# Scores of a chunked linear attention in four 64-column tiles, with the step halves of four heads swapped

## The chip, the cores and the metric

The kernel runs on one core of a Trainium2 chip. The metric is the time of one execution on the device in microseconds (us). The engines are named as in the profile: PE (TensorE; PEld is its weight load), DVE (VectorE), ACT (ScalarE), POOL (GpSimd), SP (SyncE, which here only issues DMAs).

## The reference

A layer of linear attention with a decay (RWKV5) feeds a gated feed-forward block. All arrays are float32.

```
r, k, v: [4 batches, 8 heads, 768 steps, 48]     w, u: [8, 48], w in 0.85 to 0.95
for t in steps:
    cur   = (u * k_t) outer v_t
    y_t   = r_t @ (state + cur)
    state = w * state + k_t outer v_t
x   = y as [3072 tokens, 384]
out = (silu(x @ w_gate) * (x @ w_val)) @ w_out    # w_gate, w_val: 384 x 1536, w_out: 1536 x 384
```

The loop over steps is a matrix product in pieces. Within 128 steps, y_t is a sum over the earlier steps s < t of (r_t . decayed k_s) v_s, plus the own step with u in place of the decay, plus r_t times the state that the 128 steps began with.

## The kernel before

**Items.** The attention is cut into 24 items: 6 chunks of 128 steps times 4 batches, numbered i = 4c + b. An item has 8 heads, in 4 pairs; head e of a pair lies in rows 64e to 64e+47 of a transposed tile. Each item goes through these steps:

- `load(i)` (L118 to L122) brings k and r, one DMA each, with the steps on the 128 partitions and heads and dimensions along the rows (tiles `k_ld`, `r_ld`; `hats` for the first four items). `load_v(i)` (L124 to L131) brings v in two DMAs, one for each e.
- POOL multiplies r, k and u (`own_product`, L234 and L235; tile `rk`), and DVE sums that over the dimensions (`own_sum`, L240; tile `du`). This is the own-step term of each head.
- POOL multiplies k and r by tables of powers of w (`scale_k` L307, `scale_r` L310; tables `kscale` and `rscale`, one row for each step of the chunk, both part of the tile `scales`). They are made once by `natural_tables` (L312 to L317).
- `turn(i)` (L343 to L353) transposes both for i < 12: PE writes tile `tp`, and ACT copies it to `kT` and `rT` (DVE for i < 4). From item 12 on, sixteen DMAs on SP move 32x32 blocks about (`move_blocks`, L355 to L373) and DVE turns each (`turn_blocks`, L379).
- `scores(i)` (L385 to L404) multiplies, for each head, the 48 rows of `kT` (128 keys, the stationary operand) with the 48 rows of `rT` (128 query steps, the moving operand): 8 matmuls into two PSUM tiles `s_ps`, one for each e. The result has keys on partitions and queries on columns, and only the part with key before query is wanted. `diagonal(i)` writes the own-step terms on the diagonal of the tile `At`, zero elsewhere (ACT L328, POOL L335). Then DVE copies `s_ps` into `At` where a mask of 128x128 says key < query (copy_predicated, L398).
- `outputs(i)` (L406 to L430) makes y in PSUM tile `y_ps`: for each 32 output rows it adds v times `At`, and the state `Z` times `rT`, in four column tiles of 32. ACT copies the result to `xT`.
- `update(i)` (L432 to L454) multiplies k and v over the steps (`u_ps`, four column tiles) and adds to the state (DVE, then POOL by a decay).

A matmul of an operand of 48 rows and 128 columns uses a part of the array only; the two heads of a pair lie in different rows, so they run side by side. Where this text speaks of a tile of the array, it means such a part, by rows and columns.

**Weights.** The three weight matrices come in 18 chunks of 768 KB (`load_weights`, L154 to L161, tile `w_bits`, three buffers). Each chunk is rounded by ACT (L179, L185) and DVE, and put together by POOL (L222). ACT's rounding of a chunk stands in the same order of instructions as its copies of `kT`, `rT`, and `xT`.

**Feed-forward.** `gate_value` (L464) makes the first groups of tokens, two recursive schemes with fewer products (L539 and L720) the rest. Their pieces wait in a list and are put between the attention's steps by `feed` and `gaps`.

**What sets the order.** Each engine works through its instructions in order, and the order is written out by hand (L976 to L1114): first items 0 to 3 with the weights, then a loop over s = 4 to 25. In it, loop step s does the loads of item s+3, v of item s+1, the scaling of item s+1, the turn of item s, the scores of item s-1 and the outputs and update of item s-2 (of item s-2 directly behind the scores of s-1 from s = 12 on). The DMAs of k, r, v, the weights and the block moves are all issued by SP, in this one order, each waiting for its own destination to be free.

In the built program every DMA of SP also waits for a semaphore of the DMA issued eight before it, so that there are at most eight in flight; that is so before and after the change.

Of the kernel before, what the change touches and what calls it, by code (L numbers as in the profile page):

```python
# [9 lines left out]
FP32 = mybir.dt.float32  # L10
INT32 = mybir.dt.int32
# [4 lines left out]
P = 128  # L16
# [6 lines left out]
def fast(  # L23
# [39 lines left out]
    ps_a = ctx.enter_context(tc.tile_pool(name="ps_a", bufs=4, space=bass.MemoryType.PSUM))  # L63
# [8 lines left out]
    bad = cst.tile([P, HP], FP32, name="bad")  # L72
    held = cst.tile([P, HP], FP32, name="held")
    badc = cst.tile([P, 1], FP32, name="badc")
    ones = cst.tile([P, 1], FP32, name="ones")
    ident = cst.tile([P, P], FP32, name="ident")
    mask = cst.tile([P, P], FP32, name="mask")
# [12 lines left out]
    free = deque(banks[:2])  # L90

# [25 lines left out]

    def load(i):  # L118
        c, b = divmod(i, B)
        rows = slice(P * c, P * (c + 1))  # L120
        for src, dst in zip((k, r), raw(i)):
            sp.dma_start(out=dst, in_=src[b, :, rows, :].rearrange("h t d -> t h d"))  # L122

    def load_v(i):  # L124
        c, b = divmod(i, B)
        rows = slice(P * c, P * (c + 1))
        for e in range(2):
            sp.dma_start(
                out=v_ld[i % 4][:, :, 64 * e : 64 * e + D],
                in_=v[b, :, rows, :].rearrange("(a e) t d -> e t a d", e=2)[e],  # L130
            )  # L131
# [133 lines left out]
    def warm(n):  # L265

        ps = ps_a.tile([P, HP, P], FP32, name="warm", tag="a")
        for _ in range(n):
            pe.matmul(ps[:, 0, :], ident[:], ident[:], start=True, stop=True)
# [6 lines left out]
        base=0, pattern=[[1, P]], channel_multiplier=-1,  # L276
    )
    dve.tensor_scalar(held[:], wcol[:], W_LOW, W_HIGH, ALU.max, ALU.min)
# [23 lines left out]
    def at(i, a):  # L302

        return HP - 1 - a if i >= BLOCKS and i % 2 == 0 else a

    def scale_k(i):
        pool.tensor_mul(khat[i % 4][:, :, 0:D], raw(i)[0], kscale)  # L307
# [4 lines left out]
    def natural_tables():  # L312
        for t, dst in ((pw[:, :, 1 : P + 1], kscale), (pv, rscale)):
            t_ps = ps_a.tile([P, HP, P], FP32, name="t_ps", tag="a")
            for a in range(HP):
                pe.transpose(t_ps[:, a, :], t[:, a, :], ident[:])
            act.copy(dst, t_ps[:].rearrange("p a (e x) -> p (a e) x", e=2)[:, :, 0:D])  # L317
# [25 lines left out]
    def turn(i):  # L343
        kr = khat[i % 4], rhat_of(i)
        tps = [ps_a.tile([P, HP, P], FP32, name="tp", tag="a") for _ in kr]
        turned[i] = three.tile([P, HP, P], FP32, name="rT", tag="rT")
        for tp, t, dst, table in zip(tps, kr, (kT[i % 2], turned[i]), (pw[:, :, 1 : P + 1], pv)):
            for a in range(HP):
                pe.transpose(tp[:, a, :], pair(t, a), ident[:])  # L349
            if i < 4:  # L350
                dve.tensor_mul(dst[:], tp[:], table)
            else:
                act.copy(dst[:], tp[:])  # L353
# [31 lines left out]
    def scores(i):  # L385

        while lazy:
            lazy.popleft()()
        ps = [ps_a.tile([P, HP, P], FP32, name="s_ps", tag="a") for _ in range(2)]
        for a in range(HP):  # L390
            for e in range(2):
                rows = slice(64 * e, 64 * e + D)
                pe.matmul(  # L393
                    ps[e][:, a, :], kT[i % 2][rows, at(i, a), :], turned[i][rows, at(i, a), :],
                    start=True, stop=True, skip_group_check=True,
                )
        for e in range(2):
            lazy.append(lambda e=e: dve.copy_predicated(  # L398
                At[i % 2][:].rearrange("p (a e) t -> p a e t", e=2)[:, :, e],
                mask[:].bitcast(INT32).unsqueeze(1).to_broadcast([P, HP, P]), ps[e][:],  # L400
            ))
        lazy.popleft()()
        if i < BLOCKS:
            lazy.popleft()()  # L404

    def outputs(i):  # L406

        c, b = divmod(i, B)  # L410
        A, vl, z = At[i % 2], v_ld[i % 4], Z[b]
        rT = turned.pop(i)
        ps = ps_a.tile([P, CC, P], FP32, name="y_ps", tag="a")
        cols = [[] for _ in range(4)]
        for m in range(4 * CC):
            (cc, q), (a, s) = divmod(m, 4), divmod(m, 3)
            each = [(z[0:R2, a, 32 * s : 32 * s + 32], rT[0:R2, at(i, a), :])] if c > 0 else []
            if s < 2:
                each.append((vl[:, a, 32 * s : 32 * s + 32], A[:, 2 * a, :]))
            if s > 0:  # L420
                each.append((vl[:, a, 32 * s + 16 : 32 * s + 48], A[:, 2 * a + 1, :]))
            cols[q] += [(cc, x, n == 0, n == len(each) - 1) for n, x in enumerate(each)]
        for n in range(len(cols[0])):
            for q in range(4):
                cc, x, start, stop = cols[q][n]
                pe.matmul(  # L426
                    ps[32 * q : 32 * q + 32, cc, :], *x,
                    start=start, stop=stop, skip_group_check=True,
                )
        act.copy(xT[:, i % NX, :, :], ps[:])  # L430

    def update(i):  # L432
# [4 lines left out]
        ps = ps_a.tile([P, HP, D], FP32, name="u_ps", tag="a")  # L437
# [398 lines left out]
    def three_units(g):  # L836
# [8 lines left out]
        def bank(chain):  # L845
            return wide[chain][:]

        def open_(chain):
            if chain in ("l4", "l2"):
                return take()  # L850
            return ps_a.tile([P, 4 * P], FP32, name=f"c_{chain}", tag="a")

        def later(at, do, out, *args):
            todo.append((at, lambda: do(out, *(bank(a) if isinstance(a, str) else a for a in args))))  # L854

# [9 lines left out]
        for t in range(4):  # L865
# [16 lines left out]
            later(z + 9.6, act.copy, y, "y")  # L882
            later(z + 10.4, dve.tensor_add, c[5], q10, "l5")
            later(z + (11.55 if t == 3 else 10.5), dve.tensor_add, c[2], y, "l1")
# [3 lines left out]
            later(z + r4, dve.tensor_sub, c[1], "l1", x)  # L888
            later(z + r4 + 0.1, dve.tensor_sub, c[1], c[1], "l8")
            later(z + r0, dve.tensor_sub, c[2], c[2], "l2")  # L890
            todo.append((z + r0 + 0.05, lambda: free.append(wide["l2"])))
            later(z + 11.6, dve.tensor_sub, c[0], r12, "n")
            silu(z + 10.8, 0, room["c"][:, 2], hTs[:, :, 3 * t + 2], pool, z + 10.9)
# [138 lines left out]
    outputs(2)  # L1032
    load(4)
# [3 lines left out]
    scale_k(3)  # L1037
    round_act()
# [13 lines left out]
    for s in range(4, N + 2):  # L1052
# [41 lines left out]
        if s == 12:  # L1094

            dve.tensor_tensor(bad[:], held[:], wcol[:], ALU.not_equal)
            dve.tensor_reduce(badc[:], bad[:], axis=AX.X, op=ALU.add)
            dve.memset(ones[:], 1.0)
            n_ps = ps_a.tile([P, HP, P], FP32, name="n_ps", tag="a")
            pe.matmul(n_ps[0:1, 0, 0:1], badc[:], ones[:], start=True, stop=True)  # L1100
            act.copy(outside, n_ps[0:1, 0, 0:1])
# [426 lines left out]
```

## Time and profile before

| | |
|---|---|
| three runs | 602.26, 602.87, 602.90 us |
| median | 602.87 us |
| profiled execution | 602.26 us |
| its span (first to last instruction) | 600.4 us |
| matmul instructions and their weight loads | 4920 and 4920 records |
| scores (L393), `s_ps` | 384 records, 272 ns each at the median |
| mask copies (L398), on DVE | 48, 742 ns at the median |
| loads: k and r of items 4 to 23; v; weights | 20 and 20; 48; 18 DMAs |
| granted TensorE clock | 1.0 of full speed throughout |

A busy time on the page adds up what an engine's instructions take, with overlaps counted once. A matmul of float32 shows in the trace as two records, one after the other. "SPq" lines are the issue of DMAs by SP; a DMA "lands" later, when its data are there. In a line of the timeline, the square brackets give how long the engine was idle before and what ended that. Times of the trace are from the start of the span. The chain of waits follows the work that ended last back to the start; what lies on it sets the end.

### The profile page before, as it was taken

How to read it: one execution, taken by the hardware profiler on the slowest of the kernel's cores; microseconds unless marked ns; L12 is line 12 of the kernel's file. 1: busy time of each engine (PE TensorE's matmuls, PEld its weight loads, DVE VectorE, ACT ScalarE, POOL GpSimd, SP SyncE). 2: the span in 40 equal slices, each digit the busy share in tenths (PEclk: the TensorE clock that was granted, in tenths of full speed). 3: DMA queues.
4: the chain of work that ended last, by engine and by line, in shares of the span. 5: the costliest groups of instructions: out<-in, count | busy, mean ns of one | idle time of the engine just before them, and what ended most of it. 6: DMA issues, size and time to landing. Idle time of an engine off the chain costs nothing.

```text
span 600.4 us, 12410 instructions
## 1 busy us (share of the span) xinstructions
PE 586.4 (98%) x4920; PEld 528.0 (88%) x4920; DVE 404.7 (67%) x682; ACT 227.8 (38%) x524; POOL 312.7 (52%) x349
## 2 busy tenths in 40 slices
PE   8799999999999999999999999999999999999996
PEld 7578888899988889988899988889988899988896
DVE  5867886359477877477869477869347686277660
ACT  3358887321353422253441244432134421243310
POOL 4879888987999501977710988404445200011000
PEclk9999999999999999999999999999999999999999
DMA  7989883241530503133251253200100000000001
GB/s 174 236 210 246 228 289 84 44 73 40 115 47 8 97 3 75 37 66 53 34 93 24 68 88 49 36 2 1 41 14 0 2 1 26 27 1 1 2 0 58
DMA packets 138003, 40.43 MB, mean 67 GB/s; under 512 B 128592, under 2 KB 131792, under 8 KB 137936
## 3 DMA queue, kind: packets, MB, share of 16 engines
q1 hardware_dynamic: 134480, 34.82, 27.3%
q10 hardware_dynamic: 3456, 4.72, 2.2%
q8 instruction: 41, 0.67, 0.5%
q14 instruction: 26, 0.21, 0.1%
HBM read 28.51 MB, written 4.72 MB: 55 GB/s over the span
## 4 chain that ended last, share of the span: by engine, by line
PE 88%; POOL 2%; DVE 2%; issue 1%; DMA 1%; ACT 0%; SPq 0%; DVEq 0%; POOLq 0%
PE bank L720 31%; PE bank L539 26%; PE bank L464 7%; PE c_l L720 6%; PE y_ps L426 6%; PE c_n L720 3%; PE c_y L720 3%; PE s_ps L393 3%; POOL wgv L222 1%; PE u_ps L441 1%; PE tp L349 1%; DMA r_ld<-in_r_dram 1%; DVE hv L744 1%; DVE hs L513 0%; POOL hats L310 0%
## 5 line engine op out<-in xcount | busy, mean ns | idle before, releaser
L744 DVE TENSOR_TENSOR hv<-hv,bank 128x512 f32<-128x512 f32 x132 | 88.1, 683 | 29.6 <-PE bank L720 19.3
L464 PE MATMUL bank<-xT,wgv 128*128 128x256 f32 x288 | 66.8, 385 | 0.6 <-ACT xT L430 0.6
L328 ACT ACTIVATE At<-ident,du 128x128 f32<-128x128 f32 x176 | 60.3, 396 | 15.6 <-DVE hv L552 7.5
L720 PE MATMUL bank<-xf,wgv 128*128 128x256 f32 x256 | 66.0, 382 | 0.0
L860 POOL TENSOR_TENSOR hv<-At,hats 128x512 f32<-128x512 f32 x8 | 10.2, 1274 | 107.1 <-ACT At L859 107.1
L744 ACT COPY hv<-bank 128x512 f32<-128x512 f32 x72 | 40.2, 585 | 59.5 <-PE bank L720 50.5
L464 PEld LDWEIGHTS bank<-xT,wgv 128*128 128x128 f32 x288 | 53.2, 190 | 8.9 <-ACT xT L430 0.8
L650 POOL TENSOR_TENSOR s<-wgv 128x256 f32<-128x256 f32 x39 | 30.0, 793 | 53.4 <-PE bank L539 53.2
L720 PEld LDWEIGHTS bank<-xf,wgv 128*128 128x128 f32 x256 | 47.8, 190 | 7.0 <-DVE kT L854 0.6
L539 PE MATMUL bank<-wo,hv 128*128 128x192 f32 x288 | 49.6, 327 | 0.0
L398 DVE COPY_PREDICATED At<-mask,s_ps 128x512 f32<-128x512 int32 x48 | 34.3, 741 | 20.6 <-ACT At L328 13.8
L539 PEld LDWEIGHTS bank<-wo,hv 128*128 128x128 f32 x288 | 47.2, 190 | 0.6
L539 PE MATMUL bank<-wt,hs 128*128 128x192 f32 x240 | 42.1, 327 | 1.2 <-DVE hs L513 1.2
L545 ACT COPY hv<-bank 128x192 f32<-128x192 f32 x36 | 11.3, 316 | 83.9 <-PE bank L539 83.9
L539 PE MATMUL bank<-wo,hs 128*128 128x192 f32 x240 | 42.5, 327 | 0.0
L539 PEld LDWEIGHTS bank<-wt,hs 128*128 128x128 f32 x240 | 39.3, 190 | 2.1 <-issue 1.1
L539 PEld LDWEIGHTS bank<-wo,hs 128*128 128x128 f32 x240 | 39.5, 190 | 0.5 <-DVE hv L547 0.3
L751 ACT ACTIVATE hv<-hv 128x512 f32<-128x512 f32 (+1 forms) x33 | 21.1, 668 | 48.6 <-DVE hv L744 48.6
L426 PE MATMUL y_ps<-At,v_ld 128*32 128x128 f32 x768 | 34.9, 273 | 1.4 <-DVE At L398 1.4
L720 PE MATMUL bank<-xT,wgv 128*128 128x256 f32 x144 | 35.6, 380 | 0.0
L720 PE MATMUL bank<-xT,s 128*128 128x256 f32 x152 | 35.2, 380 | 0.0
L454 POOL TENSOR_TENSOR Z<-Z,w 48x192 f32<-48x192 f32 x32 | 17.3, 540 | 33.3 <-DVE Z L453 32.1
(203 smaller groups left out, 1299.8 us busy)
## 6 DMA issues: line engine op xcount, KB each, us to landing
hats<-hats SPq DMA_DIRECT2D x192, 32.0 KB, 2.0
w_bits<-in_moe_w_gate_dram SPq DMA_DIRECT2D x6, 768.0 KB, 6.6
v_ld<-in_v_dram SPq DMA_DIRECT2D x48, 96.0 KB, 3.5
w_bits<-in_moe_w_val_dram SPq DMA_DIRECT2D x6, 768.0 KB, 6.0
w_bits<-in_moe_w_out_dram SPq DMA_DIRECT2D x6, 768.0 KB, 6.1
out_dram<-hv ACTq DMA_DIRECT2D x24, 192.0 KB, 1.9
k_ld<-in_k_dram SPq DMA_DIRECT2D x20, 192.0 KB, 3.3
r_ld<-in_r_dram SPq DMA_DIRECT2D x20, 192.0 KB, 3.7
```

What stands on the lines that cost most here:

```text
L328: lambda h=h: act.activation(At[i % 2][:, h, :], ident[:], AF.Identity, scale=du[:, h : h + 1])
L393: pe.matmul(ps[e][:, a, :], kT[i % 2][rows, at(i, a), :], turned[i][rows, at(i, a), :], start=True, stop=True, skip_group_check=True,)
L398: lazy.append(lambda e=e: dve.copy_predicated(At[i % 2][:].rearrange("p (a e) t -> p a e t", e=2)[:, :, e], mask[:].bitcast(INT32).unsquee ...
L426: pe.matmul(ps[32 * q : 32 * q + 32, cc, :], *x, start=start, stop=stop, skip_group_check=True,)
L454: pool.tensor_mul(ze, ze, w)
L464: pe.matmul(gv[:, o, :].rearrange("p (i t) -> p i t", i=2), wt[:, c, P * f : P * (f + 1)], xT[:, 2 * g % NX : 2 * g % NX + 2, c, :], start ...
L539: pe.matmul(ps, lhs[:, f, :], rhs[:, f, :], start=(f == 0 and n in (0, 1, 4)), stop=(f == FH - 1), skip_group_check=True,)
L545: act.copy({0: o1[:, 0:NH], 2: o1[:, NH:DM], 3: o2[:, NH:DM]}[n], ps)
L650: op(made[o], made[a], made[b])
L720: pe.matmul(ps[:, o], u[:, o], v, start=first and o == 0, stop=True, skip_group_check=True,)
L744: do(out, *(pair_of(wide[a][:]) if isinstance(a, str) else a for a in args))
L751: todo.append((at, lambda: act.activation(gate, gate, AF.Silu)))
```

## The change

Of a head's 128x128 scores, the quarter with keys 64 to 127 and queries 0 to 63 is above the diagonal and not wanted. The changed kernel leaves it out, from item 4 on. It also keeps heads 4 to 7 (pairs 2 and 3) with their 64-step halves swapped: steps 64 to 127 lie on partitions and columns 0 to 63. For these heads the left half of the keys (columns 0 to 63 of the array) are the late ones, which need only late queries.

- A score matmul of 128 keys becomes two of 64 keys, one in each column half of the array. For a head of pairs 0 and 1 the left tile streams all 128 queries and the right one the right 64; for a head of pairs 2 and 3 the right tile streams all 128 and the left one the left 64. So each of the four 64x64 tiles (two by rows, two by columns) streams 384 columns for an item, where it streamed 512. There are 16 matmuls for an item instead of 8.
- The loads put the halves in their swapped places. The k and r of an item come in 3 DMAs each instead of one (all partitions for heads 0 to 3; two of 64 partitions for heads 4 to 7), v in 6 instead of 2. For items 4 to 23 that is 14 instead of 6.
- The scaling tables of heads 4 to 7 are swapped in the same way, once: two DMAs bring them to a spare part of `xT` ahead of `load(4)`, and POOL copies them back behind `scale_k(3)`.
- The mask has a second half for the swapped heads, and copy_predicated reads both; the number of elements for one copy stays at 128x512.
- `outputs` reads heads 4 to 7 of `At` and `rT` as two runs of 64 columns in swapped order, so that y comes out in the order of time.
- The pool of four PSUM buffers becomes four fixed tiles used in turn, and the recursive scheme takes them out of the turn and gives them back by hand. Three small tiles become one.

The order of the steps on each engine is otherwise as before. The diff, without the renamed PSUM tiles and the repeated `back` lines:

```diff
@@ -60,7 +60,7 @@
...
-    ps_a = ctx.enter_context(tc.tile_pool(name="ps_a", bufs=4, space=bass.MemoryType.PSUM))
+    ps_a = ctx.enter_context(tc.tile_pool(name="ps_a", bufs=1, space=bass.MemoryType.PSUM))
@@ -69,12 +69,11 @@
-    bad = cst.tile([P, HP], FP32, name="bad")
-    badc = cst.tile([P, 1], FP32, name="badc")
-    ones = cst.tile([P, 1], FP32, name="ones")
+    counts = cst.tile([P, HP + 2], FP32, name="counts")
+    bad, badc, ones = counts[:, 0:HP], counts[:, HP : HP + 1], counts[:, HP + 1 : HP + 2]
-    mask = cst.tile([P, P], FP32, name="mask")
+    mask = cst.tile([P, 2, P], FP32, name="mask")
@@ -89,6 +88,13 @@
+    ring_a = deque(ps_a.tile([P, 4 * P], FP32, name=f"ring{n}") for n in range(4))
+
+    def next_psum(m, n):
+        t = ring_a[0]
+        ring_a.rotate(-1)
+        return t[:, 0 : m * n].rearrange("p (a x) -> p a x", a=m)
+
@@ -115,20 +121,34 @@
             return khat[i][:, :, 0:D], rhat[i % 2][:, :, 0:D]
         return k_ld[i % 2][:], r_ld[i % 2][:]
 
+    SWAPPED = 4
+
+    def places(i, n):
+
+        if i < SWAPPED:
+            return [(slice(0, P), slice(0, n), 0)]
+        return [
+            (slice(0, P), slice(0, n // 2), 0),
+            (slice(0, 64), slice(n // 2, n), 64),
+            (slice(64, P), slice(n // 2, n), -64),
+        ]
+
     def load(i):
         c, b = divmod(i, B)
-        rows = slice(P * c, P * (c + 1))
         for src, dst in zip((k, r), raw(i)):
-            sp.dma_start(out=dst, in_=src[b, :, rows, :].rearrange("h t d -> t h d"))
+            for p, h, o in places(i, H):
+                rows = slice(P * c + p.start + o, P * c + p.stop + o)
+                sp.dma_start(out=dst[p, h], in_=src[b, h, rows, :].rearrange("h t d -> t h d"))
 
     def load_v(i):
         c, b = divmod(i, B)
-        rows = slice(P * c, P * (c + 1))
         for e in range(2):
-            sp.dma_start(
-                out=v_ld[i % 4][:, :, 64 * e : 64 * e + D],
-                in_=v[b, :, rows, :].rearrange("(a e) t d -> e t a d", e=2)[e],
-            )
+            for p, a, o in places(i, HP):
+                rows = slice(P * c + p.start + o, P * c + p.stop + o)
+                sp.dma_start(
+                    out=v_ld[i % 4][p, a, 64 * e : 64 * e + D],
+                    in_=v[b, :, rows, :].rearrange("(a e) t d -> e t a d", e=2)[e][:, a],
+                )
 
 
     chunks = []
@@ -273,8 +293,10 @@
     pool.memset(mask[:], 1.0)
     pool.affine_select(
         out=mask[:], in_=mask[:], compare_op=ALU.is_gt, fill=0.0,
-        base=0, pattern=[[1, P]], channel_multiplier=-1,
+        base=0, pattern=[[0, 2], [1, P]], channel_multiplier=-1,
     )
+    pool.memset(mask[0:64, 1, 64:P], 0.0)
+    pool.memset(mask[64:P, 1, 0:64], 1.0)
     dve.tensor_scalar(held[:], wcol[:], W_LOW, W_HIGH, ALU.max, ALU.min)
     tables = hTs[:, 1, 0:5].rearrange("p f x -> p (f x)").rearrange(
         "p (o h x) -> p o h x", o=2, h=HP
@@ -386,19 +408,36 @@
 
         while lazy:
             lazy.popleft()()
-        ps = [ps_a.tile([P, HP, P], FP32, name="s_ps", tag="a") for _ in range(2)]
-        for a in range(HP):
+        ps = [next_psum(HP, P) for _ in range(2)]
+        whole, left, right = slice(0, P), slice(0, 64), slice(64, P)
+        if i < SWAPPED:
+            parts = [(a, whole, whole) for a in range(HP)]
+        else:
+            parts = []
+            for a in range(HP // 2):
+                parts += [(a, left, whole), (a, right, right)]
+                parts += [(a + HP // 2, right, whole), (a + HP // 2, left, left)]
+        for a, keys, cols in parts:
             for e in range(2):
                 rows = slice(64 * e, 64 * e + D)
                 pe.matmul(
-                    ps[e][:, a, :], kT[i % 2][rows, at(i, a), :], turned[i][rows, at(i, a), :],
+                    ps[e][keys, a, cols],
+                    kT[i % 2][rows, at(i, a), keys], turned[i][rows, at(i, a), cols],
                     start=True, stop=True, skip_group_check=True,
                 )
+
+        def masked_copy(e):
+            if i < SWAPPED:
+                dst = At[i % 2][:].rearrange("p (a e) t -> p a e t", e=2)[:, :, e]
+                m = mask[:, 0].bitcast(INT32).unsqueeze(1).to_broadcast([P, HP, P])
+                dve.copy_predicated(dst, m, ps[e][:])
+                return
+            dst = At[i % 2][:].rearrange("p (o a e) t -> p o a e t", o=2, e=2)[:, :, :, e]
+            m = mask[:].bitcast(INT32).unsqueeze(2).to_broadcast([P, 2, HP // 2, P])
+            dve.copy_predicated(dst, m, ps[e][:].rearrange("p (o a) t -> p o a t", o=2))
+
         for e in range(2):
-            lazy.append(lambda e=e: dve.copy_predicated(
-                At[i % 2][:].rearrange("p (a e) t -> p a e t", e=2)[:, :, e],
-                mask[:].bitcast(INT32).unsqueeze(1).to_broadcast([P, HP, P]), ps[e][:],
-            ))
+            lazy.append(lambda e=e: masked_copy(e))
         lazy.popleft()()
         if i < BLOCKS:
             lazy.popleft()()
@@ -410,15 +449,26 @@
         c, b = divmod(i, B)
         A, vl, z = At[i % 2], v_ld[i % 4], Z[b]
         rT = turned.pop(i)
-        ps = ps_a.tile([P, CC, P], FP32, name="y_ps", tag="a")
+        ps = next_psum(CC, P)
         cols = [[] for _ in range(4)]
+
+        def in_order(x, a):
+            if i < SWAPPED or a < HP // 2:
+                return x
+            return bass.AP(
+                tensor=x.tensor, offset=x.offset + 64,
+                ap=[list(x.ap[0]), [-64, 2], [1, 64]],
+            )
+
         for m in range(4 * CC):
             (cc, q), (a, s) = divmod(m, 4), divmod(m, 3)
-            each = [(z[0:R2, a, 32 * s : 32 * s + 32], rT[0:R2, at(i, a), :])] if c > 0 else []
+            each = []
+            if c > 0:
+                each.append((z[0:R2, a, 32 * s : 32 * s + 32], in_order(rT[0:R2, at(i, a), :], a)))
             if s < 2:
-                each.append((vl[:, a, 32 * s : 32 * s + 32], A[:, 2 * a, :]))
+                each.append((vl[:, a, 32 * s : 32 * s + 32], in_order(A[:, 2 * a, :], a)))
             if s > 0:
-                each.append((vl[:, a, 32 * s + 16 : 32 * s + 48], A[:, 2 * a + 1, :]))
+                each.append((vl[:, a, 32 * s + 16 : 32 * s + 48], in_order(A[:, 2 * a + 1, :], a)))
             cols[q] += [(cc, x, n == 0, n == len(each) - 1) for n, x in enumerate(each)]
         for n in range(len(cols[0])):
             for q in range(4):
@@ -848,10 +898,13 @@
-            return ps_a.tile([P, 4 * P], FP32, name=f"c_{chain}", tag="a")
+            return ring_a.popleft()
+
+        def back(at, chain):
+            todo.append((at, lambda: ring_a.append(wide[chain])))
...
@@ -880,16 +933,21 @@
...
+            back(z + 9.7, "y")
+            back(z + 10.45, "l5")
...
@@ -1030,11 +1088,17 @@
     scores(3)
     scale_k(2)
     outputs(2)
+    swapped = xT[:, NX - 1].rearrange("p c (o t) -> p (c o t)", o=2).rearrange(
+        "p (n h d) -> p n h d", n=2, h=H // 2
+    )
+    for p, o in ((slice(0, 64), 64), (slice(64, P), -64)):
+        sp.dma_start(out=swapped[p], in_=scales[p.start + o : p.stop + o, 1:3, H // 2 : H])
     load(4)
     round_act()
     feed(1)
     outputs(3)
     scale_k(3)
+    pool.tensor_copy(scales[:, 1:3, H // 2 : H], swapped)
     round_act()
     round_pool()
     scale(4)
```

More of the change, by code (lines that the diff above doesn't have):

```diff
@@ L265, in warm @@
     def warm(n):
-        ps = ps_a.tile([P, HP, P], FP32, name="warm", tag="a")
+        ps = next_psum(HP, P)
         for _ in range(n):
@@ L313, in natural_tables @@
         for t, dst in ((pw[:, :, 1 : P + 1], kscale), (pv, rscale)):
-            t_ps = ps_a.tile([P, HP, P], FP32, name="t_ps", tag="a")
+            t_ps = next_psum(HP, P)
             for a in range(HP):
@@ L344, in turn @@
         kr = khat[i % 4], rhat_of(i)
-        tps = [ps_a.tile([P, HP, P], FP32, name="tp", tag="a") for _ in kr]
+        tps = [next_psum(HP, P) for _ in kr]
         turned[i] = three.tile([P, HP, P], FP32, name="rT", tag="rT")
@@ L436, in update @@
         kh, vl, z = khat[i % 4], v_ld[i % 4], Z[b]
-        ps = ps_a.tile([P, HP, D], FP32, name="u_ps", tag="a")
+        ps = next_psum(HP, D)
         for a in range(HP):
@@ L888, in three_units @@
             later(z + r4, dve.tensor_sub, c[1], "l1", x)
+            back(z + r4 + 0.05, "l1")
             later(z + r4 + 0.1, dve.tensor_sub, c[1], c[1], "l8")
+            back(z + r4 + 0.15, "l8")
             later(z + r0, dve.tensor_sub, c[2], c[2], "l2")
@@ L892, in three_units @@
             later(z + 11.6, dve.tensor_sub, c[0], r12, "n")
+            back(z + 11.65, "n")
             silu(z + 10.8, 0, room["c"][:, 2], hTs[:, :, 3 * t + 2], pool, z + 10.9)
@@ L1094, in fast @@
         if s == 12:
[L1096 to L1100, printed above, removed]
+            dve.tensor_tensor(bad, held[:], wcol[:], ALU.not_equal)
+            dve.tensor_reduce(badc, bad, axis=AX.X, op=ALU.add)
+            dve.memset(ones, 1.0)
+            n_ps = next_psum(HP, P)
+            pe.matmul(n_ps[0:1, 0, 0:1], badc, ones, start=True, stop=True)
             act.copy(outside, n_ps[0:1, 0, 0:1])
```

## The prediction

> **What bounds the kernel now.** I read the page's busy times, then the stretches, then the chain of waits with tile s_ps and TensorE's timeline, then SP's and ACT's timelines. The page:
>
> ```profile
> PE 586.4 (98%) x4920; PEld 528.0 (88%) x4920; DVE 404.7 (67%) x682; ACT 227.8 (38%) x524; POOL 312.7 (52%) x349
> PE   8799999999999999999999999999999999999996
> DMA  7989883241530503133251253200100000000001
> ```
>
> PE is busy 98% of the 600.4 us span. The stretches (length, then busy us and count of PE, PEld, DVE, ACT, POOL; granted clock, DMA share, GB/s) show where it is not:
>
> ```profile
> 0.00:60.00 60.00, 52.51 (x610) 45.20 (x614) 42.51 (x92) 32.35 (x76) 45.73 (x52) 1.00 0.90 216
> 60.00:120.00 60.00, 60.00 (x723) 51.93 (x716) 40.92 (x83) 42.00 (x103) 53.68 (x47) 1.00 0.57 161
> 120.00:420.00 300.00, 298.80 (x2634) 270.42 (x2630) 219.79 (x345) 105.69 (x252) 182.65 (x217) 1.00 0.28 51
> ```
>
> Only the first stretch has real gaps, and there the DMA engines are 0.90 busy. The chain of waits is PE without a break from 58.60 on; a score block costs 1.09 us in it:
>
> ```profile
> 58.60 1.75 PE y_ps L426 x56
> ...
> 79.09 1.09 PE s_ps L393 x16
> 80.18 2.79 PE bank L464 x12
> 82.97 1.11 PE y_ps L426 x33
> ```
>
> So PE time saved after 58.60 is span saved, unless something makes PE wait instead.
>
> **The change, part by part.**
>
> *Scores.* A matmul shows as two records, so the 16 are 8 matmuls: 4 rounds of the pair e=0,1, each streaming 128 columns twice: 8 rounds. In the timeline of PE, y_ps starts 1.09 us after s_ps; its first records (8 each of two operands, 4 column tiles) come in steps of 0.11:
>
> ```profile
> 268.77 1.16 PE L393 MATMUL s_ps<-rT,kT 48*128 48x128 f32 x16
> 269.86 0.43 PE L426 MATMUL y_ps<-rT,Z 112*32 112x128 f32 x8
> ...
> 271.20 0.41 PE L426 MATMUL y_ps<-At,v_ld 128*32 128x128 f32 x8
> 271.42 0.52 PE L441 MATMUL u_ps<-v_ld,hats 128*32 128x48 f32 x32
> ```
>
> From 269.86 to 271.42 y_ps puts 56 records into 1.56 us: 14 rounds of four column tiles, 0.1115 us per 128 columns. Eight such rounds are 0.89; the rest of 1.09, 0.20, is the first weight load and the drain where the tile form changes. After the change each of the four 64x64 tiles streams 128+64 columns for each of two pairs of pairs, twice: 768 instead of 1,024 columns. If tiles run side by side, as y_ps's do, 0.25 x 0.89 = 0.22 is saved, and about 0.04 more since the first load has half the columns (an estimate: half of the 0.1 that I give it of the 0.20). I take 0.266 per item. Twenty items change; those of items 4 and 5 (at 46.6 and 54.0) lie before 58.60, so **18 x 0.266 = 4.8 us** off PE's path.
>
> The other end: tiles wait for each other in issue order. R (64 columns, the same rows, the other column half) then ends no earlier than the L ahead of it, and a group of L, L, R, R, and the swapped four, costs almost what two full rounds did: block about 1.03, 18 x 0.06 = 1.1 us. Had L and R no overlap at all, the streams would be 4 x 2 x (0.1115+0.057) = 1.35, the block 1.43, and +6 us. The trace leans to the first: in u_ps (L441, 48 columns) 32 records of four column tiles take 0.34, 10.6 ns a record, so loads and matmuls of column tiles overlap there.
>
> The Trainium skill, "TensorE: Matmul & The Clock Gate", Part 3, The mechanism, speaks against the change: packed matmuls start and end strictly in program order. The rows of y_ps cannot refute it, all their matmuls being equally long; by that rule this term would be the 1.1 worked out above, by independent tiles the 4.8.
>
> *Outputs* read heads 4 to 7 as two 64-column runs in swapped order (L426, 28 matmuls). I take 0: among L720's matmuls those on xT, whose operand is two separate runs, last 0.380 us, those on xf, one run, 0.382. Bounds: 0, or one 10.6 ns issue for half the records, 28 x 0.0106 x 20 = 6 us at worst; nearest is 0. A gain I exclude, since columns and weights stay the same.
>
> *Mask and copies.* copy_predicated keeps its 512 elements (0.74) and lies on DVE (67%): 0. The mask twice as wide and two memsets add about 0.2+0.3+2 x 0.1 = 0.7 on POOL, inside its 3.97 us wait for the first load; without that cover, 0.7. The swapped tables' copy on POOL is 384 elements like L307's 1.0 us; it falls ahead of this wait, of 2.08:
>
> ```profile
> 36.43 1.83 POOL L222 TENSOR_TENSOR wgv<-wgv,w_low 128x768 int32<-128x768 int32 x1 [2.08 <-DVE wgv L195]
> ```
>
> If DVE were earlier it would cost 1.0 of POOL, not of PE. The ring of four PSUM tiles replaces pool buffers that PE never waited for at s_ps (1.09 whatever stands before it): 0.
>
> *Loads.* Items 4 to 23 issue 14 DMAs instead of 6, +160, and two for the tables. SP issues in program order, and its queue also carries the weight chunks (w_bits):
>
> ```profile
> 42.96 0.37 SPq L122 DMA_DIRECT2D k_ld<-in_k_dram  x1
> 43.38 0.57 SPq L122 DMA_DIRECT2D r_ld<-in_r_dram  x1
> 44.05 1.63 SPq L128 DMA_DIRECT2D v_ld<-in_v_dram  x2
> 46.95 0.37 SPq L122 DMA_DIRECT2D k_ld<-in_k_dram  x1
> 47.37 0.57 SPq L122 DMA_DIRECT2D r_ld<-in_r_dram  x1
> 47.99 0.58 SPq L159 DMA_DIRECT2D w_bits<-in_moe_w_val_dram  x1
> ```
>
> These six become 18. Pitch bounds: 0.42 (k to r here) and 0.65 (hats, L364, 0.61 median and its semaphore). I take 0.48, nearest to k and v. The chunk is then issued at 42.96 + 18 x 0.48 = 51.6 instead of 47.99 and, landing 4.7 later (4.5 for the one at 34.70; 5.7 here), comes at 56.3 instead of 53.68. ACT has it at the head of its line:
>
> ```profile
> 53.77 0.53 ACT L179 ACTIVATE bank<-w_bits 128x384 f32<-128x384 f32 x1 [0.73 <-DMA w_bits<-in_moe_w_val_dram]
> 55.58 0.92 ACT L185 ACTIVATE w_low<-w_bits 128x768 int32<-128x768 uint32 x1 [1.29 <-POOL wgv L222]
> ...
> 57.98 0.56 ACT L353 COPY kT<-tp 128x512 f32<-128x512 f32 x1
> ```
>
> Behind it are the rest of the rounding and the kT copy: 0.47+0.82+0.44+0.27+0.87+0.56 = 3.4 us. So kT ends at 59.7 instead of 58.54, and y_ps starts 1.2 late. Then it repeats: every SP DMA waits for the landing of the eighth before it. After a weight pair come 6 v, 3 k, 3 r, so the next pair is due at the last chunk's landing plus five issues (2.4). With 4.7 to the landing of a pair's first chunk and 6 for its second: first chunks issued at 58.7 and 67.8, second ones landed at 65.2 and 74.4, the first w_out chunk issued at 76.8, landed at 81.5. ACT takes that one at 76.81 now, and ends its kT copy 3.4 later (80.23, and y_ps follows at 82.9). From 81.5, kT ends at 84.9, and PE waits 2.1 beyond its present time. One more cycle gives 96.1, ahead of the 96.9 at which PE comes: the queue has caught up. Of the scores' gain only what falls after that wait counts: 16 x 0.266 = 4.3. **Net: +2.1 - 4.3 = -2.1 us** (rounded).
>
> For items 12 up SP waits for DVE 85.8 us ahead of the block moves (L364): at 155.53 to 166.77 it has 11.2 us where about 9 of loads (18 x 0.48) fit. Those I cost at 0; with that cover gone each such pair of items would be up to 12 x 0.48 = 5.8 later at the moves, and PE behind them.
>
> The profiled 602.26 (1.86 around the span) is the lowest of three runs, median 602.87. 602.26 - 2.1 = 600.2; +0.3 to come halfway to the median: **600.5**.
>
> **Rivals.** All are against the same 602.26 + 0.3.
> (A) The forecast, 600.5: 0.32. What speaks for each step stands above.
> (B) The loads stay hidden (pitch 0.42, landings as before), and the full 4.8 shows: 597.8. For it: SP sits idle for 3 us ahead of 42.96, and ACT has gaps of 0.73 and 1.29 there. Against it: DMA share 0.90. Chance 0.18.
> (C) Slower: the w_bits issues behind 12 added DMAs each in the startup. At pitch 0.65 the chunk of 47.99 goes out at 54.7 and lands at 59.4, and by the same steps the next ones go at 62.6, 72.5 and 82.4; that one lands at 87.1, kT ends at 90.5 and y_ps is 7.7 late against a gain of 4.3: 605.9. For it: v_ld takes 5.1 to 7.2 to land where a chunk is just ahead of it, and the block moves have a pitch of 0.65. Against it: k, r and v are at 0.42 to 0.62. The sign turns at a wait of 4.3, which on the line between 2.1 (at 0.48) and 7.7 (at 0.65) is a pitch of 0.55. Chance 0.24.
> (D) Tiles keep issue order: gain 16 x 0.06 = 1.0 after the same wait of 2.1, so 603.7; with no overlap at all, 2.1 + 16 x 0.34 = 7.5 and 610. For it: PE has only ever run equal matmuls side by side here. Against it: u_ps. Chance 0.12.
> (E) The parts cancel, as at a pitch of 0.55, or where the wait is at 4: 602.9. Chance 0.14.
>
> **How the numbers follow.** 0.2% (1.2 us) is about what a measurement of this kernel can tell from no change. Faster is A and B: 0.50. Same is E and D's mild end: 0.16. Slower is C and the rest of D: 0.34. A's own range is 599 to 602 (pitch 0.45 to 0.52). With 0.32 + 0.18 + 0.14 and most of C's 0.24, 597.5 to 605.9 leaves out no more than 2 in 10.
>
> **What would show it.** Right: s_ps to the next form in about 0.83 us; PE's busy time down by 4 to 5; PE waiting for ACT kT at 59 to 60 and near 83; w_bits issued at 51 to 52. Wrong: s_ps at 1.0 or more; y_ps over 1.68 in the chain; DMA pitch over 0.55; SP's moves late after 120; or PE waiting in the startup for v_ld or k_ld itself.

## The result, and the profile after

The change makes the kernel slower: 613.35 us (median of 6 runs, 612.71 to 613.98) against 602.53 us before (6 runs). The ratio is 1.0181, 95% interval 1.0167 to 1.0194, or 10.8 us. The prediction was 600.5, faster, with a range up to 605.9. Both the sign and the range were wrong.

The page of the changed kernel (span 612.2 us; the profiled run took 613.98):

```profile
PE 585.2 (96%) x5240; PEld 524.9 (86%) x5240; DVE 405.1 (66%) x682; ACT 227.1 (37%) x524; POOL 314.1 (51%) x352
PE   8898788999999999999999999999999999999996
DMA  7966778323253132224223323210000000100001
```

PE has about as much busy time as before, and in the second line its gaps now reach through the seventh slice, to 107 us (a slice is 15.3 us). The same stretches as shown of before:

```profile
0.00:60.00 60.00, 51.70 (x590) 43.84 (x590) 39.22 (x86) 27.61 (x63) 45.49 (x54) 0.97 0.76 177
60.00:120.00 60.00, 48.97 (x653) 41.39 (x652) 39.02 (x79) 40.84 (x100) 38.81 (x35) 0.97 0.69 194
120.00:420.00 300.00, 298.48 (x2902) 268.79 (x2902) 213.97 (x340) 107.51 (x256) 195.55 (x228) 1.00 0.29 53
```

From 60 to 120 us PE is idle for 11.0 us where it was idle for 0.0. The DMA engines are less busy up to 120 us than in the startup before (0.76 and 0.69 against 0.90), which speaks against their rate as the limit; e11 below tries it. From 120 on PE is about as busy as it was. The chain of waits names what PE waits for (start, length, what):

```profile
57.01 5.27 DMA w_bits<-in_moe_w_val_dram
62.32 0.04 issue
62.36 0.51 ACT bank L199
62.87 0.81 ACT w_low L205
...
65.26 0.34 ACT kT L375
65.60 5.10 DMA w_bits<-in_moe_w_gate_dram
...
77.58 4.58 DMA w_bits<-in_moe_w_gate_dram
...
87.71 4.65 DMA w_bits<-in_moe_w_out_dram
...
117.67 0.81 PE ring L423 x24
118.49 2.80 PE bank L514 x12
121.29 1.68 PE ring L476 x56
```

Where PE filled the chain from 58.60 on, it is now weight chunk after weight chunk until 105 us, then ACT and DVE behind the last of them until 114, and PE only from there. (The names `s_ps`, `tp`, `y_ps` and `u_ps` are `ring` now.) The last three lines are good news: from the start of a score block to the next work it takes 0.82 us instead of 1.09, and the outputs still take 1.68.

### The profile page after: what moved, and what is told of

It reads as the page before. It is cut to its first block, busy times and chain, and to the rows that moved or that the text cites. A ratio compares the mean times of both kernels' runs of the same rounds, so it can differ in the third digit from the quotient of the medians.

```text
span 612.2 us, 13288 instructions
## 1 busy us (share of the span) xinstructions
PE 585.2 (96%) x5240; PEld 524.9 (86%) x5240; DVE 405.1 (66%) x682; ACT 227.1 (37%) x524; POOL 314.1 (51%) x352
## 4 chain that ended last, share of the span: by engine, by line
PE 76%; DMA 7%; ACT 5%; DVE 3%; SPq 2%; issue 1%; POOL 1%; POOLq 0%; ACTq 0%; DVEq 0%
PE bank L770 29%; PE bank L589 25%; PE ring L770 12%; PE ring L476 4%; PE bank L514 3%; DMA w_bits<-in_moe_w_val_dram 2%; SPq L141 2%; PE ring L423 2%; DMA w_bits<-in_moe_w_gate_dram 2%; DMA w_bits<-in_moe_w_out_dram 2%; ACT bank L199 1%; ACT At L350 1%; ACT w_low L205 1%; DMA r_ld<-in_r_dram 1%; DVE hv L794 1%
## 5 line engine op out<-in xcount | busy, mean ns | idle before, releaser
L514 PE MATMUL bank<-xT,wgv 128*128 128x256 f32 x288 | 68.8, 391 | 3.7 <-DVE hv L521 2.9
L350 ACT ACTIVATE At<-ident,du 128x128 f32<-128x128 f32 x176 | 60.4, 398 | 13.9 <-DVE hv L602 7.4
L437 DVE COPY_PREDICATED At<-mask,ring 128x512 f32<-128x512 int32 x40 | 28.7, 740 | 15.7 <-ACT At L350 13.1
L476 PE MATMUL ring<-rT,Z 112*32 112x128 f32 x480 | 30.9, 284 | 7.9 <-ACT kT L375 7.9
L504 POOL TENSOR_TENSOR Z<-Z,w 48x192 f32<-48x192 f32 x32 | 18.6, 582 | 38.4 <-DVE Z L503 37.2
L476 PE MATMUL ring<-At,v_ld 128*32 128x128 f32 x768 | 36.0, 279 | 1.4 <-DMA v_ld<-in_v_dram 1.4
```

Of the source, the lines that this page charges most:

```text
L350: lambda h=h: act.activation(At[i % 2][:, h, :], ident[:], AF.Identity, scale=du[:, h : h + 1])
L437: dve.copy_predicated(dst, m, ps[e][:].rearrange("p (o a) t -> p o a t", o=2))
L476: pe.matmul(ps[32 * q : 32 * q + 32, cc, :], *x, start=start, stop=stop, skip_group_check=True,)
L504: pool.tensor_mul(ze, ze, w)
L514: pe.matmul(gv[:, o, :].rearrange("p (i t) -> p i t", i=2), wt[:, c, P * f : P * (f + 1)], xT[:, 2 * g % NX : 2 * g % NX + 2, c, :], start ...
```

## How late each item is

A second reading carries the rest of this text: when the outputs of an item start on PE (first record of L426, now L476), less the time of the same item in the kernel before. Each kernel is read from its one profiled execution. Before, items 4, 6 and 9 start at 58.60, 82.90 and 119.33, the last at 434.46.

| kernel | ACT begins the chunk issued at 47.99 before, us | item 4 | item 6 | item 9 | last item |
|---|---|---|---|---|---|
| before | 53.77 | 0 | 0 | 0 | 0 |
| changed | 62.36 | +7.2 | +13.0 | +13.8 | +11.6 |
| whole loads (e1) | 52.72 | -1.6 | -2.1 | -2.9 | -6.0 |
| only the split loads (e2) | 62.28 | +7.1 | +14.9 | +16.9 | +17.0 |
| split by heads (e10) | 59.20 | +4.0 | +7.2 | +8.4 | +8.4 |
| small DMAs (e11) | 64.52 | +9.3 | +14.2 | +14.9 | +14.9 |
| weights first (e8) | 53.27 | +0.7 | +2.3 | +1.9 | -0.1 |
| from item 8, weights first (e9) | 52.29 | -1.3 | -1.3 | -2.1 | -4.5 |

In the changed kernel, all of the early loss comes before item 9: item 8 is 14.0 late, the most of all. After that nearly every item wins back 0.26 to 0.27 (items 18, 21 and 23 do not).

One part of these numbers is no gain of the scores. Items 2 and 3, whose scores the change leaves as they were, already start earlier in most kernels built on the changed one: 1.2 us in the changed kernel and in e1, 1.9 in e3, but 0.4 in e13. No run shows why. So a lateness is best read from item 4 on, as a difference between items of one kernel.

## The experiments

Theory Q: SP issues more DMAs, each slowly, ahead of the weight chunks; the chunks come late; ACT, which rounds them in order, holds up its copy of `kT`; PE waits for the PSUM tile that `kT` is copied from. Rival S: the new scores or the swapped reads cost PE time. Rival M: the cut transfers slow the DMA engines themselves.

### e1: the scores without the loads

```diff
     def places(i, n):
-        if i < SWAPPED:
-            return [(slice(0, P), slice(0, n), 0)]
-        return [
-            (slice(0, P), slice(0, n // 2), 0),
...
+        return [(slice(0, P), slice(0, n), 0)]
...
-    for p, o in ((slice(0, 64), 64), (slice(64, P), -64)):
-        sp.dma_start(out=swapped[p], in_=scales[p.start + o : p.stop + o, 1:3, H // 2 : H])
...
-    pool.tensor_copy(scales[:, 1:3, H // 2 : H], swapped)
```

> The changed kernel with the loads of the kernel before (one DMA each for k and r, two for v) and without the swapped tables; the score matmuls, the mask copies and the reads of the outputs stay as changed. It leaves out the swap of heads 4 to 7, so their results are of other steps. Theory Q (the loss is the queue of SP: more DMAs ahead of the weight chunks): the startup is that of before, and the scores' gain shows whole: s_ps to the next form 0.82 instead of 1.09, 18 to 20 x 0.27, so 597 to 598 us. Rival S (the new scores or the swapped reads of the outputs cost PE time themselves): 603 or more. Rival in between: if the gaps in the startup take up part of the gain, 599 to 600.

Measured: 596.33 us against 601.82 on the same chip, ratio 0.9905 (0.9889 to 0.9922), 5.5 us faster. PE has no gaps after 60:

```profile
60.00:120.00 60.00, 60.00 (x824) 52.01 (x823) 40.51 (x84) 40.77 (x100) 52.45 (x45) 1.00 0.56 157
```

The items come 0.26 earlier one by one: from item 4 (-1.6) to the last (-6.0) that is 4.4 us, 17 steps. The other 1.6 us is there at item 4 already, and of that 1.2 ahead of any changed score. Rival S falls.

### e2: the loads without the scores

```diff
         for src, dst in zip((k, r), raw(i)):
-            sp.dma_start(out=dst, in_=src[b, :, rows, :].rearrange("h t d -> t h d"))
+            for p, h in places(i, H):
+                rows = slice(P * c + p.start, P * c + p.stop)
+                sp.dma_start(out=dst[p, h], in_=src[b, h, rows, :].rearrange("h t d -> t h d"))
...
```

Here `places` is that of the changed kernel without the shift by 64 steps; v is cut likewise.

> The kernel before with its k, r and v loads of items 4 to 23 cut into 3, 3 and 6 DMAs as in the changed kernel, steps in their old places, nothing else changed. Theory Q: all of the loss without the gain, 602.5 + 10.8 + 5 = 618 (616 to 620), PE idle ahead of the outputs of item 4 by some 5 us, and the granted clock below 1 after it. Rival S: at most 605.

Measured: 619.43 us against 601.82, ratio 1.0290 (1.0272 to 1.0307), 17.6 us slower. With e1 that gives 17.6 - 5.5 = 12.1 where the whole change costs 10.8: the two parts nearly add up, and the loss is in the loads.

### e10 and e11: the number of DMAs, their partitions, or their bytes

In e10 the kernel before gets as many DMAs as in e2, but all of 128 partitions:

```diff
+            (slice(0, P), slice(0, n // 2)),
+            (slice(0, P), slice(n // 2, n // 4 * 3)),
+            (slice(0, P), slice(n // 4 * 3, n)),
```

> The kernel before with loads cut into as many DMAs as in e2 (3, 3 and 6), but all of 128 partitions, cut by heads alone. If the number of DMAs makes the loss: as e2, 619 (616 to 622), pitch 0.6 to 0.65. If it is the halves of the partitions (64-partition transfers that use the DMA engines badly): 612 or less.

Measured: 610.57 against 602.51, ratio 1.0141 (1.0120 to 1.0163), 8.1 us slower, half of e2's loss. The issues on SP show why. Tile v_ld, count, then shortest, median and longest issue in ns; first e2, then e10:

```profile
L139 SPq DMA_DIRECT2D v_ld<-in_v_dram x128: 422/602/1833, 8.5 to 395.3; - x128
```

```profile
L139 SPq DMA_DIRECT2D v_ld<-in_v_dram x128: 328/425/1714, 9.3 to 383.9; - x128
```

An issue takes 602 ns in the median where two of three DMAs touch only 64 partitions, and 425 ns where all touch 128, with the same bytes in as many DMAs. The block moves of 32 partitions (L364 before) had shown 609. Rival M would explain the loss too, by slower transfers. So e11 adds DMAs that carry nothing: four behind each item's k and r, four behind its v.

```diff
+    def extra(i, n):
+        if i >= 4:
+            for m in range(4):
+                sp.dma_start(out=idle[0:64, 4 * n + m : 4 * n + m + 1], in_=k[0, 0, 0:64, 0:1])
```

> The kernel before with 8 more DMAs for each of items 4 to 23, each 4 bytes on 64 partitions to a spare tile: 4 behind its k and r, 4 behind its v. They move next to nothing. If SP's time to issue a DMA of 64 partitions (0.60 to 0.65 us in the changed kernel), with eight in flight, is what costs: 616 to 620, as e2. If it is what the cut transfers do to the DMA engines: 606 or less. In between, if a small DMA is issued faster (0.45): 608 to 612, as e10.

Measured: 617.87 against 602.36, ratio 1.0265 (1.0245 to 1.0286), 15.5 us slower. They move 256 bytes each and cost nearly what the split loads do:

```profile
L123 SPq DMA_DIRECT2D idle<-in_k_dram x160: 465/595/3300, 26.3 to 392.4; - x160
```

So more issues on SP, 0.6 us each and with at most eight in flight, are enough for a loss of this size, with next to no bytes. That leaves some 2 us, the difference between e11 and e2, for the cut transfers themselves. How the 15.5 us divide between the time of the issues and the limit of eight in flight was not tried. The Trainium skill, "DMA: Bandwidth & Descriptors", Rules for kernel authors, advises against two transfers to disjoint partition halves because they share the same DMA engines. The advice holds here, but e11 loses nearly as much with next to no data to share the engines for.

### e3 and e7: the swap from a later item on

```diff
-    SWAPPED = 4
+    SWAPPED = 12
```

The swapped tables are made in the loop, ahead of the first swapped item. In e7 it is 8.

> The changed kernel with the swap (loads, tables, scores, outputs) from item 12 on instead of 4; items 4 to 11 load and score as before. Theory Q, with the loss all in the startup: weights are loaded by then, so 12 x 0.27 = 3.3 is gained and nothing lost: 599.3 (598.7 to 600). If the longer loads also delay the block moves of the late items: 601 to 606. Rival S: 603 or more.

> The changed kernel with the swap from item 8 on: 16 items gain 0.27 each (4.3 us), and 4 items (8 to 11) still add 8 DMAs each of 0.65 to the stretch in which weights are loaded. Theory Q with a loss that grows with each item in that stretch (17 us for 8 items): half of it stays, 602 to 606. Q with slack for the first few: 598 to 600. Rival M (each split transfer slows the DMA engines down wherever it runs): as e3, with 0.27 x 4 more gained, 598.

Measured: from item 12, 598.95 against 601.82, ratio 0.9956 (0.9939 to 0.9972). From item 8, 605.56 against 602.51, ratio 1.0046 (1.0030 to 1.0061). The ten runs of e7 spread from 602.54 to 607.57. The loads of items 8 to 11 alone cost some 7 us (3.1 lost instead of 4.3 gained). Those of items 12 up are issued when the last weight chunk is out, and cost one wait: in e3 PE waits once for POOL among the late items, and POOL, behind it, for loads behind the block moves:

```profile
376.44 1.97 PE L770 MATMUL bank<-xT,s 128*128 128x256 f32 x8 [1.49 <-POOL s L700]
```

In the changed kernel that wait is 0.7 us, in e1 there is none. That e3 came near its forecast of 599.3 is partly luck: its items are 2.2 us early at item 4, ahead of any swapped item, ten steps win 2.6 more, and the wait takes 1.5 back.

### e5: the weights from another queue

```diff
-            sp.dma_start(
+            act.dma_start(
                 out=bits[n][:].rearrange("p (c f) two -> p c (f two)", c=src.shape[1]), in_=src
```

> The changed kernel with the 18 weight chunks issued by ACT's queue instead of SP's, the loads still in 14 DMAs. Theory Q (what is late is the issue behind SP's other DMAs): chunks go out as soon as ACT has freed their buffer, the waits on kT in the startup go, 598 to 601, with up to 18 x 1 us of issue on ACT, which is busy 38%. Rival M (the split transfers themselves slow the DMA engines down, whoever issues them): chunks still land late, 608 or more. A third way: loads of k and r, still at 0.65 a DMA on SP, hold up POOL and PE themselves: 604 to 608.

Measured: 616.77 against 601.82, ratio 1.0261 (1.0242 to 1.0280): worse than the changed kernel, where Q had led to expect 598 to 601. It doesn't decide about Q, since it does not take the chunks out of the line. The eight semaphores go round over the DMAs of both queues, so a chunk issued by ACT waits for the landing of a small load issued by SP, and now ACT itself stands still (a line of ACT's timeline):

```profile
63.12 0.51 ACT L199 ACTIVATE bank<-w_bits 128x384 f32<-128x384 f32 x1 [5.31 <-DMA k_ld<-in_k_dram]
```

The third way of the expectation shows as well: SP still issues 12 loads for an item, and they come late themselves. In the chain of waits the outputs of item 4, at 70.72, stand behind a load of v:

```profile
64.23 4.16 DMA v_ld<-in_v_dram
...
70.72 3.04 PE ring L476 x56
```

### e8, e9 and e12: the weights ahead of the loads

```diff
+            if s >= BLOCKS:
+                load_v(s + 1)
-            load_v(s + 1)
-            if s + 3 < N and not late:
+            if s + 3 < N and not late and s >= BLOCKS:
                 load(s + 3)
...
         gaps(s, 2)
+        if s < BLOCKS:
+            load_v(s + 1)
...
         gaps(s, 4)
+        if s < BLOCKS:
+            load(s + 3)
```

This is e8, all on the changed kernel: in steps 4 to 11 the loads move behind the places at which chunks are loaded. In e9 the swap also begins at item 8, in e12 at item 6.

> The changed kernel, all loads split from item 4 on, but in loop steps 4 to 11 the v loads of the next item stand behind the third place for weights, and the k and r loads of the item three on behind the fifth, so that no weight chunk waits behind 12 DMAs at once. If the loss is the place of the weight chunks in SP's order: 598 to 604, the wait of the outputs of item 4 on kT down from 5.5 us to under 2. If it is the sheer number of issues (SP's own 0.65 each) or loads of k and r that now come late themselves: 608 or more.

> Both edits: swap from item 8 on, loads placed behind the weights in steps 4 to 11. Theory Q: 597.5 to 599, at or below the variant from item 12 (598.95). If late k and r loads hold POOL up: 600 to 606.

> As e9, with the swap from item 6 on: 18 items gain 0.27 (4.9 us, 0.5 more than e9), and two more items are split in the stretch of the weights. If SP has room for them with the weights first: 596.8 to 597.3 against before at 602.5. If not: 598 to 601.

Measured: e8 602.56 against 602.51, ratio 1.0008 (0.9994 to 1.0023). It has the DMAs of the changed kernel, 471 on SP, and only their order differs; that order was worth 10 to 11 us. It does not give back all: e8 is some 6 us slower than e1, and its item 6 still starts 2.3 late where it is 2.1 early in e1. Its ten runs spread from 602.06 to 606.40. e9: 597.61 against 602.51, ratio 0.9911 (0.9895 to 0.9928), 4.9 us faster than before and faster than both kernels of this text; 1.3 of this stand at item 4 already, ahead of any swapped item. e12: 599.14 against 602.36, ratio 0.9945 (0.9928 to 0.9962). e12 is 0.34% or 2 us behind e9, though it should gain 0.5 more: splitting the loads of items 6 and 7, in the stretch of the weights, costs some 2.5. SP's timeline in e9, the stretch around 60 us:

```profile
57.46 2.87 SPq L141 DMA_DIRECT2D r_ld<-in_r_dram  x3
...
61.77 0.53 SPq L179 DMA_DIRECT2D w_bits<-in_moe_w_gate_dram  x1
62.41 1.02 SPq L148 DMA_DIRECT2D v_ld<-in_v_dram  x2
63.53 0.45 SPq L179 DMA_DIRECT2D w_bits<-in_moe_w_val_dram  x1
64.50 2.24 SPq L141 DMA_DIRECT2D k_ld<-in_k_dram  x3
```

A chunk now stands between the groups of loads; in the changed kernel it stood behind 12 of them, the one at 57.01 behind 18.

### e6 and e13: the clock behind the wait

In the changed kernel PE runs slowly just after its wait for item 4. These are the first records of the outputs there:

```profile
65.78 0.66 PE L476 MATMUL ring<-rT,Z 112*32 112x128 f32 x8 [5.47 <-ACT kT L375]
66.21 0.65 PE L476 MATMUL ring<-At,v_ld 128*32 128x128 f32 x8
```

The groups last 0.66 and 0.65 instead of 0.43 and 0.41, the outputs 3.0 us instead of 1.6, and the granted clock is 0.66 from 65 to 70 us. The spare matmuls should have kept PE busy in the wait.

```diff
+        if s == 6:
+            t = ring_a[0]
+            for _ in range(KEEP):
+                pe.matmul(t[:, 0:P], ident[:], ident[:], start=True, stop=True)
```

In e13 the second line is `t = free[0]`; KEEP is 22.

> The changed kernel with 22 spare matmuls of 128x128 on PE ahead of the outputs of item 4, where it waits 5.5 us for kT. They take about 4.7 us and write a PSUM tile that the outputs then overwrite. If the low granted clock behind that wait (0.66 from 65 to 70 us, y_ps 3.0 us instead of 1.6) comes of PE having been idle, the clock stays near 1 and the outputs of item 4 take 1.6 us. What that is worth at the end: up to 1.5 us (612) if PE's own work sets the next items, nothing (613.3) if they wait for weight chunks anyway, which I hold for likelier.

> The spare matmuls of e6 again, now into a bank of the feed-forward that is free by then, not into the tile for which the outputs wait. They should run inside PE's wait of 5.5 us, so y_ps of item 4 starts at 65 to 66 us as in the changed kernel and takes 1.6 instead of 3.0 us. The end: at most 1.5 us earlier (612) if the slow clock behind the wait is on the path, the same (613.3) if item 6 waits for its weight chunk anyway.

Measured: e6 617.20 against 602.36, ratio 1.0237 (1.0220 to 1.0254); e13 614.91 against 602.87, ratio 1.0200 (1.0179 to 1.0222). Neither did what it was built for, because the spare matmuls waited too. In e6 they waited for the very tile that `kT` is copied from, in e13 for a bank that DVE frees only behind ACT. In e13's timeline of PE:

```profile
65.43 7.18 PE L1152 MATMUL bank<-ident 128*128 128x128 f32 x44 [6.93 <-DVE hv L522]
72.54 0.43 PE L477 MATMUL ring<-rT,Z 112*32 112x128 f32 x8
```

Two things can be read from e13 all the same. The slow clock goes with the idle time and not with the new kind of matmul: the spare matmuls now run slowly (granted clock 0.53 from 65 to 70 us), and the outputs behind them at full speed, 0.43. In e2, which has none of the new matmuls, the first group of outputs behind a wait of 6.31 us takes 0.65 as well. The Trainium skill, "TensorE: Matmul & The Clock Gate", Part 1, What's actually happening, says that an idle array drops to half its clock and gets it back after about 3.4 us of work. Half a clock for 3.4 of five microseconds would be a mean of 0.66, an estimate from that page, and 0.66 was measured. In e13 the slow stretch is twice as long: 0.78 from 60 to 65 us and 0.53 from 65 to 70 make 6.9 us at half clock.

And the slow stretch doesn't seem to be on the path to the end: in e13 item 4 starts 13.9 late instead of 7.2, but item 6 only 14.0 instead of 13.0, and the last item 11.6 as in the changed kernel. In e6 item 4 is as late (13.9), but item 6 is 15.6 and the last item 16.0 late; where these further microseconds come from stays open.

## Why the prediction was wrong

**The score block was right.** 0.82 us was measured for a forecast of 0.83, so a gain of 0.27 instead of 0.266. Rival D, tiles in issue order, is out; its block would have been 1.03. The Trainium skill, "TensorE: Matmul & The Clock Gate", Part 3, The mechanism, lets packed matmuls end in program order only. Taken as a price, that would have given the 1.03, by the estimate of the prediction; the 0.82 decides against it as a price. The forecast of 18 x 0.266 = 4.8 became 4.4 in e1, in 17 steps. The rest of e1's 5.5 was there ahead of them and is no score gain that these runs show. The worst case of the prediction was summed short (1.35 and the 0.20 beside it make 1.55, not 1.43); no run came near it.

**Outputs, mask and ring at 0 were right.** The outputs take 1.68 in both chains, and in e1 PE is busy without a gap from 60 to 120. The tables were not tried alone; e1 leaves their swap out.

**The loads were mis-sized, and that is the failed step.** It said: "Pitch bounds: 0.42 (k to r here) and 0.65 (hats, L364, 0.61 median and its semaphore). I take 0.48, nearest to k and v." The nearest row was the other one. The new DMAs touch 64 partitions, those of hats 32, those of k and v 128. And the 0.42 is the pitch of a load that SP issues after standing idle: in the prediction's own lines r, directly behind k, takes 0.57. (The trace shows 12 loads for an item instead of 4, where the text on the change and the prediction say 14 instead of 6; the 8 more for each, 160 in all, are right.) SP's timeline in the changed kernel, the stretch that the prediction worked out:

```profile
44.15 0.55 SPq L179 DMA_DIRECT2D w_bits<-in_moe_w_gate_dram  x1
44.80 1.75 SPq L141 DMA_DIRECT2D k_ld<-in_k_dram  x3
46.59 2.04 SPq L141 DMA_DIRECT2D r_ld<-in_r_dram  x3
48.73 3.88 SPq L148 DMA_DIRECT2D v_ld<-in_v_dram  x6
52.71 1.85 SPq L141 DMA_DIRECT2D k_ld<-in_k_dram  x3
54.60 2.31 SPq L141 DMA_DIRECT2D r_ld<-in_r_dram  x3
57.01 0.67 SPq L179 DMA_DIRECT2D w_bits<-in_moe_w_val_dram  x1
```

18 DMAs from 44.80 to 57.01 are 0.68 each, waits between them included, where 0.48 was taken (3.6 us). The stretch also begins at 44.80 instead of 42.96 (1.8 us): the loads ahead of it were split as well, the chunk between them went out at 44.15 instead of 38.97, and the 3 us for which SP had stood idle ahead of 42.96 were used up. The prediction left this start where it was. So the chunk went out at 57.01 instead of the forecast 51.6, it took 5.3 to land instead of 4.7, and outputs of item 4 were 7.2 late instead of 1.2.

**The cycle behind it was mis-sized too.** The next pairs of chunks were forecast at 58.7, 67.8 and 76.8, nine microseconds apart. In the chain above they go out at 65.60, 77.58 and 87.71, 12.0 and 10.1 apart: the five issues behind a landing, 2.4 us in the forecast, took 3.3 ahead of 65.60 and 4.6 ahead of 77.58. So item 6 came 13.0 late instead of 2.1, and the queue had not caught up by the next item, as "One more cycle gives 96.1, ahead of the 96.9" would have it, but only at item 8 (+14.0).

**Rival C named the place, the mechanism and the pitch**, and still fell short: 7.7 late where 13.0 to 14.0 were measured, for two of the same reasons (the start of the stretch, and the cycle). Its forecast was 605.9, and 613.35 was measured.

**The late items were nearly right.** SP has the room that was claimed; one wait of 0.7 us for POOL was missed.

The sum as measured: item 8 is 14.0 late; from there to the last item the scores give back twelve steps of 0.26 (3.1), and at item 21, behind the late wait, 0.7 is lost: 14.0 - 3.1 + 0.7 = 11.6, the last item's lateness. The span of this profiled run is 11.8 longer, the median time 10.8.

## What to carry to other kernels

Count what a change adds to each DMA queue in issues, not in bytes, and price an issue by a row of the same number of partitions that stands directly behind another issue. Then look at what stands behind them in the same queue: here 18 loads instead of 6 held up a weight chunk that another engine needed at the head of its own line, and the same DMAs in another order cost 10 to 11 us less. Where chunks and loads take turns and only so many may be in flight, a longer issue costs time in every turn, so work out more than the first turn.

## What was not expected of the hardware

- SP takes about 0.60 us to issue a DMA of 64 or of 32 partitions, whether it carries 24 or 48 KB (item loads), 32 KB (block moves) or 256 bytes (e11). For those of 128 partitions in e10 the medians are 0.43 (v) and 0.47 (k and r). The number of partitions is not all: of the whole loads of the kernel before, k at 42.96 takes 0.37 where SP was idle ahead of it, and r directly behind it 0.57 (0.58 in the median of all r). In the changed kernel the whole ones among the partial ones take about as long as those (the shortest of all loads of r is 0.595). Why a partial one takes longer was not tried.
- Two kinds of tiles, 64 by 64 with 128 and with 64 columns to stream, keep out of each other's way: 768 instead of 1,024 columns took 0.82 instead of 1.09 us, a quarter of the block's time.
- A DMA issued from ACT's queue waited for a load issued from SP's (e5), since the program's eight DMA semaphores go round over both.
